# The head of a fused attention and MLP kernel: all first loads on one queue, w1 in smaller pieces, two transposed tiles copied in halves, layer 1 in a new order

## The chip, the cores and the metric

One NeuronCore of a Trainium2 chip runs the whole kernel. The metric is the device time of one execution in microseconds (us). The core has TensorE (PE in the profile; its weight loads are PEld), VectorE (DVE), ScalarE (ACT), GpSimd (POOL) and SyncE (SP), which does nothing here but issue DMAs. ACT and POOL can issue DMAs too, each on a queue of its own. Every engine runs its own list of instructions in order; they wait for each other by semaphores.

## The reference

Two branches read the same layer-normalised input, and their sum is added to it. The sequence has S = 2048 rows of D = 448; there are 16 heads of 28 features, and the hidden layer has 1792 features; all tensors are bf16.

```
xn  = layernorm(x)
# A: linear attention with a softmax feature map
q, k, v = split(xn @ wqkv)                        # 16 heads of 28
phi(t)  = concat(softmax(t @ w_phi), softmax(-t @ w_phi))
kv, z   = sum_s phi(k)^T v,  sum_s phi(k)
A       = (phi(q) @ kv) / (phi(q) @ z + 1e-6) @ wo
# B: MLP
B       = silu(xn @ w1) @ w2
out     = x + A + B
```

## The kernel before

The rows are cut into 16 tiles of 128. A tile is normalised on DVE: statistics (`bnst`, L690, then `bnag`, L691), the reciprocal of the standard deviation (`ve` and `rstd`), and the scaling itself (`xn`, L705). For tiles 0 to 3 `ve` is a square root on ACT (L694) and `rstd` a reciprocal on DVE (L696); for the later tiles both are on POOL (L699, L701). The normalised tile must be transposed, since TensorE contracts over partitions. Tiles 0 to 3 are transposed by TensorE (`tr`, L525) into PSUM and copied to `xnT` (`ev`): by ACT (L531) for tiles 0 to 2, by DVE (L535) for tile 3. Tile 0 goes in two halves (`tr0a`/`ev0a` and `tr0`/`ev0`). Tiles 4 to 15 are transposed two at a time by DMA (`xnT_dma5`, `xnT_dma7` ... `xnT_dma15`, L613), issued by SP once DVE has written both tiles of the pair.

Layer 1 of the MLP makes blocks F0 to F27. A block is 256 hidden features (two PSUM banks) by 512 rows (four tiles); F0 to F6 are the seven feature pairs of tiles 0 to 3, and F25 belongs to tiles 12 to 15. Block F*n* with *n* below 7 needs columns 256*n* to 256*n*+255 of w1. The contraction over 448 is three full steps of 128 (the third differs between the two banks) and a rest of 64, which the two banks share. The first three blocks are made tile by tile as tiles come in, in 128x128 matmuls (the "head"); a word such as `20` is block F2 on tile 0, `00a` the first two steps of block F0 on tile 0 and `00b` its third. After the head the blocks' rests (`r0`, `r1`, `r2`) and whole blocks follow in the order of the string `PLAN` (L361), `aF3` and `bF3` being the halves of F3, `av4` a value projection of tiles 4 and 5, and so on. TensorE's order is that string to the end of the kernel, word for word; the other engines' order comes from a list scheduler (`schedule`) with estimated durations, and where a `chain` is written out, from that.

The loads of the start are all listed at L590 to L610. SP issues the x tiles (`x0`, `x1`, `x2` for tiles 2 and 3, `x4` for 4 to 7, `x8`, `x12`), the pieces of w1, wv and then the transposing DMAs of wqkv (`wT_dma`). The first 512 columns of w1 come as two DMAs: contraction steps 0 and 1 (`w1_0`) and the other two (`w1_0r`). The next columns come as three steps and a last one, so `w1_512` and `w1_512r`, `w1_1024` and `w1_1024r`; `w1_512` is on ACT's queue, behind the small activation that loads ACT's first table, and its last step is on SP's. In the profile w1 carries the name of the buffer that holds it, `phT<-in_B_w_dram`. POOL issues four small DMAs of w_phi (`Wp`), from which it then builds two masked blocks (`bdphi`, L620, and `bd0`, L624) before or between the `ve` and `rstd` of tile 4.

What orders the head is written out: TensorE by this list, ACT by a chain, and DVE by another chain that the change leaves alone.

```
chain("bnst0 bnag0 bnst1 bnag1 rstd0 xn0a xn0 rstd1 xn1 bnst2 bnag2 bnst3 bnag3 rstd2 xn2 rstd3 xn3 ev3".split())
chain("warm_act w1_512 ve0 ve1 ev0a ev0 ev1 ve2 ve3 ev2 silu_table".split())
for word in "tr0a tr0 tr1 00a 10a 01a 11a 00b 10b 01b 11b tr2 20 21 tr3 02 12 22 03 13 23".split():
```

Ahead of the head TensorE runs 38 matmuls on a constant (L574) that nothing reads.

Of the kernel before, what the change touches and what calls it, by code (L numbers as in the profile page):

```python
# [140 lines left out]
class _Prog:  # L141
# [86 lines left out]
    def schedule(self, stalls=()):  # L228
# [53 lines left out]
        while done < n:  # L282
# [78 lines left out]
PLAN = """r0 aF3@4 r2 r1 bF3 aF6@0 aF4@6 bF6 bF4 aF5@4 av2@2 av0@0 bv2 bF5 av4@6 bv0 bv4 aF10@2 aF9@0 bF10 f0@6 bF9 aF12@4 aF7@2  # L361
# [9 lines left out]
def bass_parallel_sum__linear_kernel_hedgehog__dense_activation_silu__prompt_kernel(  # L371
# [36 lines left out]
    with es:  # L408
# [171 lines left out]
        def load_x(t0, t1):  # L580
            load(x_sb[:, t0:t1, :], rows_of(A_x, t0, t1), f"x{t0}", lat=1400.0)
# [7 lines left out]

        load_x(0, 1)  # L590
        load_x(1, 2)
        load_x(2, 4)
        load(w1_sb[:, 0:2, 0:512], B_w1[0:256, 0:512].rearrange("(k p) f -> p k f", p=128), "w1_0")
        load(w1_sb[:, 2:4, 0:512], bass.AP(B_w1.tensor, B_w1.offset + 256 * FF, [[FF, 128], [64 * FF, 2], [1, 512]]), "w1_0r")
        load_w1(512, 1024, "act")
        load_x(4, 8)
        load_w1(1024, FF)
        load_rows4(wv_sb, A_wqkv, 2 * D, 3 * D, "wv")
        load_x(8, 12)
        load_x(12, 16)  # L600
# [86 lines left out]
        def ln_tile(t):  # L687
# [26 lines left out]
                          xn_sb[:, sl - 1:sl + 1, :].rearrange("p i c -> p (i c)"), 950.0, f"xnT_dma{t}", 1330.0, lat=850.0)  # L714
                return

            def turn_over(k0, k1, b, tag):
                tps = bank16[b][:, 128 * k0:128 * k1].rearrange("p (k c) -> p k c", k=k1 - k0)
                transposes([(tps[:, kt - k0, :], xn_sb[:, sl, KS[kt]:KS[kt] + 128]) for kt in range(k0, k1)], f"tr{tag}")
                if t < 3:  # L720
                    act(dstx[:, k0:k1, :], tps, ACTF.Identity, 128 * (k1 - k0), f"ev{tag}")
                else:
                    copy(dstx[:, k0:k1, :], tps, 128 * (k1 - k0), f"ev{tag}")
# [299 lines left out]

        head = [F(0, 0), F(1, 2), F(2, AUX)]
        seq = []
        for word in "tr0a tr0 tr1 00a 10a 01a 11a 00b 10b 01b 11b tr2 20 21 tr3 02 12 22 03 13 23".split():
            if word[0] == "t":
                seq.append(word)
                continue
            f, t = int(word[0]), int(word[1])  # L1030
            n0 = len(P.ops)
            head[f][0](t * 128, t * 128 + 128, {"": (0, 1, 2), "a": (0, 1), "b": (2,)}[word[2:]])
            for n, o in enumerate(P.ops[n0:]):
                o.name = f"F{word}_{n}"
                seq.append(o.name)
# [204 lines left out]
```

## Time and profile before

| | |
|---|---|
| time, median of 3 runs | 146.54 us (146.45 to 146.69) |
| span of the profiled execution, first to last instruction | 145.1 us |
| PE busy | 141.6 us (98%) |
| DVE, ACT, POOL busy | 89.5, 79.4, 75.1 us |
| granted TensorE clock | 1.00 throughout |
| DMA moved | 17.59 MB, 121 GB/s over the span |

The profile is of one execution; its own time is known as its span, and the timed runs lie 1.4 us above that, for what comes before the first and after the last instruction. A row of the timeline gives the start, the length, the engine, the line and operation, `out<-in`, the number of instructions merged, and in brackets how long the engine was idle before and what ended that. Matmuls are pipelined, so a row's start says more than its length. Times are in us from the span's start.

### The profile page before, as it was taken

How to read it: one execution, taken by the hardware profiler on the slowest of the kernel's cores; microseconds unless marked ns; L12 is line 12 of the kernel's file. 1: busy time of each engine (PE TensorE's matmuls, PEld its weight loads, DVE VectorE, ACT ScalarE, POOL GpSimd, SP SyncE). 2: the span in 40 equal slices, each digit the busy share in tenths (PEclk: the TensorE clock that was granted, in tenths of full speed). 3: DMA queues.
4: the chain of work that ended last, by engine and by line, in shares of the span. 5: the costliest groups of instructions: out<-in, count | busy, mean ns of one | idle time of the engine just before them, and what ended most of it. 6: DMA issues, size and time to landing. Idle time of an engine off the chain costs nothing.

```text
span 145.1 us, 4509 instructions
## 1 busy us (share of the span) xinstructions
PE 141.6 (98%) x1947; PEld 83.6 (58%) x1947; DVE 89.5 (62%) x195; ACT 79.4 (55%) x96; POOL 75.1 (52%) x93
## 2 busy tenths in 40 slices
PE   7999999999999999999999999999999999999994
PEld 7895444445444544476787655565555555555663
DVE  1969898600760069939049999927796384625822
ACT  4567856479995999979887949228620000000000
POOL 8808567620197008799935999991497600000000
PEclk9999999999999999999999999999999999999999
DMA  4999998746970000000000069959889999633432
GB/s 101 347 346 266 283 153 119 147 87 139 356 203 5 0 2 5 0 0 5 0 5 5 0 88 195 124 108 181 76 164 164 214 193 167 134 74 72 133 127 63
DMA packets 44500, 17.59 MB, mean 121 GB/s; under 512 B 37040, under 2 KB 44096, under 8 KB 44480
## 3 DMA queue, kind: packets, MB, share of 16 engines
q1 hardware_dynamic: 41648, 15.10, 52.7%
q10 hardware_dynamic: 2704, 2.17, 5.3%
q8 instruction: 15, 0.25, 0.8%
q14 instruction: 5, 0.04, 0.1%
q0 software_dynamic: 128, 0.03, 0.1%
HBM read 6.57 MB, written 1.84 MB: 58 GB/s over the span
## 4 chain that ended last, share of the span: by engine, by line
PE 93%; DMA 3%; SPq 1%; DVE 0%; issue 0%
PE psum L508 93%; DMA phT<-in_B_w_dram 3%; SPq L545 1%; PE psum L525 0%; DVE x_sb L988 0%
## 5 line engine op out<-in xcount | busy, mean ns | idle before, releaser
L508 PE MATMUL psum<-xnT,phT 64*128 64x512 bf16 (+1 forms) x428 | 46.9, 350 | 0.3 <-ACT xnT L531 0.2
L508 PE MATMUL psum<-w_sb,hT 64*128 64x448 bf16 (+2 forms) x434 | 46.1, 343 | 0.0
L825 DVE TENSOR_REDUCE Rec<-Ek_sb 128x32 f32<-128x896 bf16 (+1 forms) x20 | 24.4, 1251 | 19.0 <-ACT Ek_sb L531 19.0
L531 ACT ACTIVATE hT<-psum 128x1024 bf16<-128x1024 f32 x28 | 27.7, 1023 | 11.2 <-PE psum L508 11.0
L508 PEld LDWEIGHTS psum<-xnT,phT 64*128 64x128 bf16 (+1 forms) x428 | 22.5, 95 | 18.5 <-ACT vaug L531 0.6
L508 PEld LDWEIGHTS psum<-w_sb,hT 64*128 64x128 bf16 (+1 forms) x434 | 23.2, 94 | 17.2 <-issue 0.2
L861 POOL TENSOR_TENSOR RA<-Ek_sb,Rec 128x896 bf16<-128x896 bf16 x16 | 27.1, 1724 | 6.1 <-DVE Rec L826 5.0
L508 PE MATMUL psum<-Wqk,xnT 64*128 64x432 bf16 x224 | 24.4, 343 | 0.0
L531 ACT ACTIVATE Ek_sb<-psum 128x864 bf16<-128x864 f32 x24 | 20.3, 915 | 5.9 <-PE psum L508 3.7
L835 POOL TENSOR_TENSOR Ek_sb<-Ek_sb,Rec 128x896 bf16<-128x896 bf16 x8 | 13.4, 1699 | 17.7 <-DVE Rec L826 17.6
L508 PEld LDWEIGHTS psum<-Wqk,xnT 64*128 64x128 bf16 x224 | 11.2, 95 | 8.1
L531 ACT ACT_TABLE_LOAD x11 | 14.1, 1283 | 1.7 <-PEq L1225 0.8
L835 POOL TENSOR_TENSOR phT<-phT,Rec 128x896 bf16<-128x896 bf16 x8 | 13.4, 1699 | 1.2 <-issue 0.9
L988 DVE TENSOR_TENSOR x_sb<-psum,x_sb 128x448 bf16<-128x448 f32 (+1 forms) x13 | 7.2, 584 | 9.1 <-PE psum L508 9.1
L508 PE MATMUL psum<-wv,xnT 64*128 64x448 bf16 x112 | 12.2, 349 | 0.0
L690 DVE BATCH_NORM_STATS2 st<-x_sb 128x6 f32<-128x448 bf16 x16 | 9.6, 603 | 2.9 <-DMA x_sb<-in_A_x_dram 2.9
L508 PE MATMUL psum<-wo_sb,vaug 64*128 64x448 bf16 (+1 forms) x102 | 10.7, 338 | 0.0
L705 DVE TENSOR_SCALAR RA<-x_sb,mv,rstd 128x384 bf16<-128x384 bf16 (+4 forms) x29 | 9.0, 348 | 1.6 <-POOL rstd L701 1.5
L967 DVE TENSOR_TENSOR vaug<-psum,rden 128x448 bf16<-128x448 f32 x16 | 9.2, 619 | 0.0
L825 DVE TENSOR_REDUCE Rec<-phT 128x64 f32<-128x1792 bf16 x4 | 8.0, 1990 | 1.9 <-ACT phT L531 1.9
L826 DVE RECIPROCAL Rec<-Rec 128x32 f32<-128x32 f32 (+1 forms) x24 | 8.8, 396 | 0.2
L508 PEld LDWEIGHTS psum<-wv,xnT 64*128 64x128 bf16 x112 | 5.3, 94 | 5.6 <-ACT vaug L531 0.5
(60 smaller groups left out, 109.7 us busy)
## 6 DMA issues: line engine op xcount, KB each, us to landing
out_dram<-x_sb ACTq DMA_DIRECT2D x15, 112.0 KB, 2.4
w_sb<-in_B_w_dram SPq DMA_DIRECT2D x1, 1568.0 KB, 7.9
x_sb<-in_A_x_dram SPq DMA_DIRECT2D x3, 448.0 KB, 6.0
wo_sb<-in_A_wo_dram SPq DMA_DIRECT2D x2, 336.0 KB, 7.5
phT<-in_B_w_dram SPq DMA_DIRECT2D x1, 576.0 KB, 7.0
phT<-in_B_w_dram SPq DMA_DIRECT2D x2, 256.0 KB, 4.4
phT<-in_B_w_dram ACTq DMA_DIRECT2D x1, 384.0 KB, 4.6
wv<-in_A_wqkv_dram SPq DMA_DIRECT2D x1, 336.0 KB, 7.2
```

Source lines behind the costliest of these rows:

```text
L508: r = e.matmul(dst, lhsT, rhs, start=st, stop=sp, skip_group_check=True)
L531: P.op("act", d_act(n), lambda e: e.activation(dst, src, func, scale=scale), reads=[src], writes=[dst], table=table, name=name, **keys)
L545: P.dma(lambda e: e.dma_start(out=dst, in_=src), n / 280.0, writes=[dst], name=name, eng=eng, lat=lat)
L690: P.op("dve", 590, lambda e: e.bn_stats(st6[:, t, :], xs), reads=[xs], writes=[st6[:, t, :]], name=f"bnst{t}", okeys_w=["ln"])
L705: P.op("dve", dur, lambda e: e.tensor_scalar(dst, x_sb[:, t, c0:c1], mv[:, t, 0:1], rstd[:, t:t + 1], ALU.subtract, ALU.mult), reads=[xs, ...
L825: P.op("dve", 50 + 967 * n, lambda e: e.tensor_reduce(R2, E4, AXL.X, ALU.add), reads=[E4], writes=[R2], name="Ssum")
L826: P.op("dve", 135 + 210 * n, lambda e: e.reciprocal(R2, R2), reads=[R2], writes=[R2], name="Rrec")
L835: P.op("pool", 1700, lambda e: e.tensor_tensor(E3, E3, Rk[:, :, None].broadcast_to([128, 32, DH]), ALU.mult), reads=[E3, Rk], writes=[E3], ...
L861: P.op("pool", 1700, lambda e: e.tensor_tensor(dst, Eq, Rq.rearrange("p (c j) -> p c j", c=CC)[:, :, :, None].broadcast_to([128, CC, 4, DH ...
L967: P.op("dve", 620, lambda e: e.tensor_tensor(o3, U3[:, :, 0:DH], rden[:, uq, :, None].broadcast_to([128, H, DH]), ALU.mult), reads=[U3[:, ...
L988: P.op("dve", d_dve(cs.stop - cs.start), lambda e: e.tensor_tensor(res[:, cs], ob, addend[:, cs], ALU.add), reads=[ob, addend[:, cs]], wri ...
```

## The change

The loads: `w1_0` is issued ahead of `x2` instead of behind it, `w1_512` moves from ACT to SP, and the columns of w1 from 512 on come in pieces of 256, 512 and 512 columns instead of 512 and 768. Each piece is two DMAs, so SP issues three DMAs more than before, all ahead of wv, x8 and the transposing DMAs; ACT issues one less. The copies out of PSUM of tiles 1 and 2 are cut in two (steps 0 and 1, then 2 and 3), and ACT's chain places `ve2` and `ve3` between them. TensorE's list does the third step of tile 0 before tile 1, puts `tr3` between `20` and `21`, and takes tile 2 by halves. In `PLAN` the blocks F4, F5, F6 come in that order instead of F6, F4, F5, in the same banks. The `lat` values are estimates for the scheduler. As built, the order of DVE is unchanged; on POOL `bd0` now stands ahead of tile 4's `ve` instead of behind it; TensorE has the same instructions in the new order.

```
-PLAN = """r0 aF3@4 r2 r1 bF3 aF6@0 aF4@6 bF6 bF4 aF5@4 av2@2 av0@0 bv2 bF5 ...
+PLAN = """r0 aF3@4 r2 r1 bF3 aF4@0 aF5@6 bF4 bF5 aF6@4 av2@2 av0@0 bv2 bF6 ...
...
         load_x(0, 1)
         load_x(1, 2)
+        load(w1_sb[:, 0:2, 0:512], B_w1[0:256, 0:512].rearrange("(k p) f -> p k f", p=128), "w1_0", lat=1200.0)
         load_x(2, 4)
-        load(w1_sb[:, 0:2, 0:512], ..., "w1_0")
-        load(w1_sb[:, 2:4, 0:512], ..., "w1_0r")
-        load_w1(512, 1024, "act")
+        load(w1_sb[:, 2:4, 0:512], ..., "w1_0r", lat=1200.0)
+        load_w1(512, 768)
         load_x(4, 8)
-        load_w1(1024, FF)
+        load_w1(768, 1280)
+        load_w1(1280, FF)
         load_rows4(wv_sb, A_wqkv, 2 * D, 3 * D, "wv")
...
-            def turn_over(k0, k1, b, tag):
+            def turn_over(k0, k1, b, tag, cut=None):
...
+                for a, b, part in ((k0, k1, ""),) if cut is None else ((k0, cut, "a"), (cut, k1, "")):
+                    if t < 3:
+                        act(dstx[:, a:b, :], tps[:, a - k0:b - k0, :], ACTF.Identity, 128 * (b - a), f"ev{tag}{part}")
...
-                turn_over(0, 4, (7, 4, 5)[t - 1], str(t))
+                turn_over(0, 4, (7, 4, 5)[t - 1], str(t), 2 if t < 3 else None)
...
-        chain("warm_act w1_512 ve0 ve1 ev0a ev0 ev1 ve2 ve3 ev2 silu_table".split())
-        byname = {o.name: o for o in P.ops}
-        byname["w1_512"].deps.add(byname["warm_act"].id)
-        byname["w1_512"].odeps -= byname["w1_512"].deps
+        chain("warm_act ve0 ve1 ev0a ev0 ev1a ve2 ev1 ve3 ev2a ev2 silu_table".split())
...
-        for word in "tr0a tr0 tr1 00a 10a 01a 11a 00b 10b 01b 11b tr2 20 21 tr3 02 12 22 03 13 23".split():
+        for word in "tr0a tr0 tr1 00a 10a 00b 10b 01a 11a 01b 11b tr2 20 tr3 21 02a 12a 22a 02b 12b 22b 03 13 23".split():
```

More of the change, by code (lines that the diff above doesn't have):

```diff
@@ L360 @@
           ("pool", "pe"): 100.0}
-PLAN = """r0 aF3@4 r2 r1 bF3 aF6@0 aF4@6 bF6 bF4 aF5@4 av2@2 av0@0 bv2 bF5 av4@6 bv0 bv4 aF10@2 aF9@0 bF10 f0@6 bF9 aF12@4 aF7@2
+PLAN = """r0 aF3@4 r2 r1 bF3 aF4@0 aF5@6 bF4 bF5 aF6@4 av2@2 av0@0 bv2 bF6 av4@6 bv0 bv4 aF10@2 aF9@0 bF10 f0@6 bF9 aF12@4 aF7@2
 aF11@0 f1@6 bF11 bF7 bF12 aF25@0 ak2@6 bF25 bk2 av8@4 av12@2 bv8 ak0@0 bv12 bk0 av10@6 aF22@4 bv10 aF17@2 bF22 av14@6
@@ L591, in bass_parallel_sum__linear_kernel_hedgehog__dense_activation_silu__prompt_kernel @@
         load_x(1, 2)
+        load(w1_sb[:, 0:2, 0:512], B_w1[0:256, 0:512].rearrange("(k p) f -> p k f", p=128), "w1_0", lat=1200.0)
         load_x(2, 4)
-        load(w1_sb[:, 0:2, 0:512], B_w1[0:256, 0:512].rearrange("(k p) f -> p k f", p=128), "w1_0")
-        load(w1_sb[:, 2:4, 0:512], bass.AP(B_w1.tensor, B_w1.offset + 256 * FF, [[FF, 128], [64 * FF, 2], [1, 512]]), "w1_0r")
-        load_w1(512, 1024, "act")
+        load(w1_sb[:, 2:4, 0:512], bass.AP(B_w1.tensor, B_w1.offset + 256 * FF, [[FF, 128], [64 * FF, 2], [1, 512]]), "w1_0r", lat=1200.0)
+        load_w1(512, 768)
         load_x(4, 8)
-        load_w1(1024, FF)
+        load_w1(768, 1280)
+        load_w1(1280, FF)
         load_rows4(wv_sb, A_wqkv, 2 * D, 3 * D, "wv")
@@ L715, in ln_tile @@
                 return
-            def turn_over(k0, k1, b, tag):
+            def turn_over(k0, k1, b, tag, cut=None):
                 tps = bank16[b][:, 128 * k0:128 * k1].rearrange("p (k c) -> p k c", k=k1 - k0)
                 transposes([(tps[:, kt - k0, :], xn_sb[:, sl, KS[kt]:KS[kt] + 128]) for kt in range(k0, k1)], f"tr{tag}")
[L720 to L723, printed above, removed]
+                for a, b, part in ((k0, k1, ""),) if cut is None else ((k0, cut, "a"), (cut, k1, "")):
+                    if t < 3:
+                        act(dstx[:, a:b, :], tps[:, a - k0:b - k0, :], ACTF.Identity, 128 * (b - a), f"ev{tag}{part}")
+                    else:
+                        copy(dstx[:, a:b, :], tps[:, a - k0:b - k0, :], 128 * (b - a), f"ev{tag}{part}")
             if t == 0:
```

## The prediction

> **What bounds the kernel now.** I read the page's busy time first, then the chain of work that ended last in order of time, then the timeline of the first 10 us, then the DMAs of the start by queue. Page, and the chain (start, length, what):
>
> ```profile
> span 145.1 us, 4509 instructions
> ...
> PE 141.6 (98%) x1947; PEld 83.6 (58%) x1947; DVE 89.5 (62%) x195; ACT 79.4 (55%) x96; POOL 75.1 (52%) x93
> ...
> PE 93%; DMA 3%; SPq 1%; DVE 0%; issue 0%
> ```
>
> ```profile
> 2.68 5.04 DMA phT<-in_B_w_dram
> 7.71 0.04 issue
> 7.76 0.62 PE psum L508 x8
> 8.38 0.22 PE psum L525 x4
> 8.60 0.67 PE psum L508 x12
> 9.27 0.22 PE psum L525 x4
> 9.50 30.98 PE psum L508 x345
> 40.48 0.01 issue
> 40.48 102.59 PE psum L508 x1503
> ```
>
> The reader is to see that TensorE has no hole from 7.76 to 143.1 and that the same instructions run after the change. So the time falls by as much as TensorE reaches its gapless stretch earlier, unless something later then makes it wait. What starts that stretch is one DMA, issued at 2.68 and landed at 7.71: w1_0r. The timeline of the head shows the rest:
>
> ```profile
> 5.70 0.35 PEld L525 LDWEIGHTS psum<-ident,RA 128*128 128x128 bf16 x4 [0.24 <-DVE RA L705]
> ...
> 7.00 0.45 PEld L508 LDWEIGHTS psum<-xnT,phT 128*128 128x128 bf16 x8 [0.38 <-ACT xnT L531]
> ...
> 7.37 0.40 DVE L705 TENSOR_SCALAR RA<-x_sb,mv,rstd 128x448 bf16<-128x448 bf16 x1
> ...
> 7.75 0.45 PEld L508 LDWEIGHTS psum<-xnT,phT 128*128 128x128 bf16 x8 [0.30 <-DMA phT<-in_B_w_dram]
> 7.87 0.40 DVE L705 TENSOR_SCALAR RA<-x_sb,mv,rstd 128x448 bf16<-128x448 bf16 x1
> 8.16 0.27 PEld L525 LDWEIGHTS psum<-ident,RA 128*128 128x128 bf16 x4
> ```
>
> TensorE stands still for tile 1's copy (until 7.00) and for w1_0r (until 7.75). The weights of tr2 are loaded at 8.16 though xn2 was done at 7.37+0.40 = 7.77. So the two waits together cost 0.4 us: what tr2 comes later than its own input allows.
>
> **Why w1_0r lands at 7.71.** The DMAs by queue between 5.0 and 5.5 (packets, MB, share; q1 is SP's, q10 ACT's):
>
> ```profile
> q10 hardware_dynamic: 164, 0.17, 96.1%
> q1 hardware_dynamic: 16, 0.01, 7.8%
> ```
>
> For half a microsecond ACT's w1_512, which nobody needs before 8.4, pushed SP's queue aside. From 6 to 7, with ACT's done, SP's queue alone moved 0.36 MB in a microsecond.
>
> **The change, part by part.** Landings of before are issue start plus the median to landing: x2 1.74+2.7 = 4.4, w1_0 5.9, w1_512 6.9, w1_0r 7.7, w1_512r 8.1, x4 9.7, w1_1024 11.2.
>
> *Loads.* On one queue 704 KB now lie up to the end of x2 and 960 KB up to the end of w1_0r. For x2: from below, 448 KB were there at 4.4 and 256 KB more at 0.36 MB/us take 0.7: 5.1; from above, the 704 KB of before were there at 5.9, with ACT's traffic between. DVE comes to bnst2 at 5.57, so the cost is 0 to 0.35; I take 0, since ACT's traffic is what goes. For w1_0r: 5.1+0.7 = 5.8 from below, the unchanged 7.7 from above; I take 5.9. For w1_768r, 2176 KB: between 1920 KB at 9.7 and 2496 KB at 11.2 it is 10.4; aF3 wants it at 11.67−0.40 = 11.27, so nothing is waited for. Rest of w1: 2688 KB, 11.7 as before, wanted by aF5 after 13.
>
> *TensorE and ACT.* 00a starts at 6.11 behind tr1, as now. Matmuls of 128 columns follow each other at 0.056 us (chain: 12 in 0.67). 00a and 10a are 8: 6.64. 00b and 10b need ev0 (the ACT row 5.55+1.40 holds ev0a, ev0, ev1; ev0 ends at 6.21) and w1_0r (5.9): 4 matmuls, 6.86. 01a and 11a need ev1a, which starts at 6.35 as ev1 does now and takes 0.38 like ev0a: 6.73. 8 matmuls, 7.31. 01b and 11b need ev1's second half: ev1a 6.35, ve2 6.63, ev1 6.84 to 7.22 (an instruction on ACT starts 0.1 before the end of the one ahead: a half takes 0.28 of it, a ve 0.2): 7.53. Then tr2 waits for xn2 until 7.76 and starts at 7.82, by tr1's distance of 0.056 from its xn1. Before it started at 8.22. **Gain 0.40.** xn2 itself cannot move: DVE's chain is unchanged, and rstd2 follows bnag3 (6.95+0.18 = 7.13), not ve2.
>
> From tr2 to the end of the head 56 matmuls at 0.056 stand on both sides. tr3, now ten matmuls behind tr2, comes at 8.38; xn3 ends at 8.27 and allows 8.32: no wait, by 0.05. ev2a and ev2 (8.25 and 8.53, 0.38 each) are there for 8.93 and 9.60. A tile in two halves takes ACT 0.28+0.28 instead of 0.50, so 0.06 more, hidden in the 1.18 us that it is idle before ev2. ACT's DMA issue of 0.43 lay in 1.53 us of idleness: 0.
>
> *SP's three more issues* at 0.47 (the median of its w1 issues) put wT_dma4 and all behind it 1.4 us later. The landing need not follow: wT_dma4 was issued by 8.5 and landed at 15.4 (8.1 after its start), so the data queue was 7 us behind the issues. Cost between 0 and 1.4 for xnT_dma5; I take 0, nearest to that row. The issue of wv moves 1.4 too; it is wanted at 16.9 and landed at 12.7.
>
> *POOL.* bd0 ahead of ve4 makes rstd4 0.05 later (bdphi ends 11.17, bd0 0.27, ve4 0.23, against 11.60 now); from below, tile 4's statistics come 0.4 earlier with ev3. The LN chain thus moves by +0.05 to −0.4; I take +0.05, as bdphi waits for Wp and that row I leave:
>
> ```profile
> 10.61 0.56 POOL L620 TENSOR_TENSOR BD<-Wp,mask_half 128x224 bf16<-128x224 bf16 x1 [3.88 <-DMA Wp<-in_A_w_phi_dram]
> ```
>
> The next fixed date is xnT_dma15, landed at 25.80+3.8 = 29.6; aF25 loads its weights at 29.90 and multiplies at 30.12, in the new kernel at 29.50 and 29.72. After w1_0r's landing TensorE needed 0.05; 29.65+0.05 = 29.70, just in time: 0 (at most 0.2). *F4, F5, F6* have equal durations: 0.
>
> **Sum** on the profiled span: 145.13 − 0.40 = 144.73. The median of the runs is 1.41 above the span: 146.54 − 0.40 = **146.14**.
>
> **The rivals.**
> 1. *x2 too late.* At its upper bound of 5.9 DVE's chain, and with it tr2, moves 0.35; the gain is 0.05: 146.5. The same is left if aF25 or another fixed date takes 0.2 back (146.35). For it: x2 now lies behind 256 KB. Against: ACT's 384 KB are gone.
> 2. *w1_0r not earlier* (the other side). It is now needed by 00b, at 6.64, ahead of all of tile 1. If it still lands at 7.71, the 16 matmuls from 00b to 11b start at 7.76, take 0.89, and tr2 comes at 8.65: 0.43 slower, 146.97. It decides from a landing at 7.28 on; up to 6.88 it costs nothing. Against: the queue rows above. The Trainium skill, "DMA: Bandwidth & Descriptors", section "Issuing engines are not separate DMA queues", says that DMAs of all issuing engines run on the same 16 engines and interleave, and that a second issuing engine saves issue time alone. By that rule alone the move to SP wins nothing at the landing; the trace agrees on the sharing, but its 164 packets to 16 show that who shares matters.
> 3. *SP late.* If all 1.4 us reach xnT_dma5, it lands at 18.9+1.4 = 20.3; av4 starts at 20.03−0.40 = 19.63, waits 0.7, and the kernel is 0.3 slower: 146.85.
> 4. *Small pieces.* If a piece carries a cost of its own on the queue, w1_768r is late: aF3 has 11.27−10.4 = 0.87 to spare. x0 and x1 landed 0.48 apart (2.87 and 3.35), the two pieces of wv 0.3 apart, the later of each 112 KB. If each of the three extra pieces cost a whole 0.48, aF3 would wait 1.44−0.87 = 0.57: 146.7; with the difference, 0.18 each, nothing waits. The Trainium skill, same page, section "Bandwidth", asks for DMAs of 1 MiB and gives 0.95 us for one of 64 KB; by that an estimate is 3x0.95−0.87 = 2.0 of waiting and 148.1. The 0.3 us of wv's second piece, which lay in a full queue as these do, disagrees.
>
> **How the numbers follow.** The forecast has 0.56, rival 1 0.20, rival 2 0.12, rival 3 0.08, rival 4 0.03; 0.01 is for no change at all. A measurement of this kernel tells about 0.2% (0.29 us) from no change. The forecast's own range is 146.0 to 146.3, and 0.03 of its 0.56 is within 0.2%. Rival 1 is within it for 0.15 and faster for 0.05; rivals 2 and 3 are slower but for 0.02 near the deciding point; rival 4 is slower for 0.01. Faster 0.58, same 0.23, slower 0.19. The range goes from 145.9 (the forecast less the 0.24 by which runs differ) to 146.85, rival 3; the later landings of rival 2 and what lies below 145.9 are left out.
>
> **What would show it.** In the profile after: w1_0r and x2 landed before 6.6 and 5.6; no DMA in the head's chain of waits but the x loads; PEld waiting for DVE before tr2, at 7.8 instead of 8.16; one gapless PE from there; wv and xnT_dma5 landed as before. Wrong it would be made by x2's statistics starting after 5.6, a PE gap before 00b, aF3, av4 or aF25.

## The result, and the profile after

| | kernel before | changed kernel |
|---|---|---|
| median of the runs made side by side | 147.22 us (146.33 to 148.40) | 147.94 us (147.16 to 149.22) |
| ratio, 95% interval | | 1.0061 (1.0033 to 1.0088) |
| span of the profiled execution | 145.1 us | 147.8 us (its time: 149.01) |
| PE busy | 141.6 us | 141.9 us |

The change makes the kernel 0.6% slower; a gain of 0.40 us had been forecast, from 146.54 to 146.14. Runs of either kernel spread over some 2 us and the median of the kernel before moves between 146.4 and 147.2 from one set of runs to the next, so every ratio below is against runs of the kernel before in the same set. The ratio is not the quotient of the two medians, and can lie up to 0.3% beside it.

On the page of the changed kernel, the shares of the span in the chain of work that ended last (before, PE had 93% of it):

```profile
PE 85%; DMA 8%; SPq 4%; DVE 1%; issue 1%
```

The chain itself (start, length, what):

```profile
5.19 7.88 DMA phT<-in_B_w_dram
13.08 0.14 issue
13.21 28.82 PE psum L508 x308
...
133.76 4.29 DMA vaug<-vaug
138.05 0.14 issue
138.19 7.53 PE psum L508 x62
```

TensorE does the same work, but it is no longer the chain from 7.76 on. Two DMAs stand in it: w1_768r, issued at 5.19 and landed at 13.08, and the last transposing DMA of the kernel, 4.29 us long. The timeline of the start says what the head itself did:

```profile
4.11 0.63 DVE L691 BATCH_NORM_STATS2 st<-x_sb 128x6 f32<-128x448 bf16 x1 [0.44 <-DMA x_sb<-in_A_x_dram]
...
6.25 0.63 DVE L691 BATCH_NORM_STATS2 st<-x_sb 128x6 f32<-128x448 bf16 x1
...
8.36 0.23 PEld L525 LDWEIGHTS psum<-ident,RA 128*128 128x128 bf16 x4 [0.34 <-DVE RA L706]
...
11.63 0.56 POOL L621 TENSOR_TENSOR BD<-Wp,mask_half 128x224 bf16<-128x224 bf16 x1 [4.93 <-DMA Wp<-in_A_w_phi_dram]
...
12.62 0.23 POOL L700 TENSOR_SCALAR ve<-mv 128x1 f32<-128x1 f32 x1 [0.19 <-DVE mv L692]
...
13.21 0.61 PE L508 MATMUL psum<-xnT,phT 64*128 64x512 bf16 x4 [1.23 <-DMA phT<-in_B_w_dram]
```

x2's statistics start at 6.25 instead of 5.57, so tr2 comes at 8.36 and not at 7.82. Most of these 0.68 us are not x2's: x1, whose issue the change leaves at 1.3, is in at 4.08 instead of 3.35, so DVE starts tile 1's statistics at 4.11 instead of 3.65 and has scaled tile 1 some 0.48 later; x2, in at 6.23, adds the other 0.20. aF3 stands still until 13.2. bdphi on POOL starts a microsecond later than before (11.63 against 10.61), and here tile 4's ve waits longer still, until 12.62, for the statistics of x4, which is in at 11.66 instead of 9.69.

I followed the same matmul through both traces. The changed kernel's TensorE is 0.15 us behind at the end of the head, 1.54 after aF3, stays there until 130, and is 2.65 behind at the end. 2.65 is far more than the 0.72 between the medians, so one pair of profiles could not settle what the change costs.

### The profile page after: what moved, and what is told of

The parts are those of the page before. It is cut to its first block, busy times and chain, and to the rows that moved or that the text cites. A ratio compares the mean times of both kernels' runs of the same rounds, so it can differ in the third digit from the quotient of the medians.

```text
span 147.8 us, 4516 instructions
## 1 busy us (share of the span) xinstructions
PE 141.9 (96%) x1947; PEld 84.4 (57%) x1947; DVE 89.6 (61%) x195; ACT 79.8 (54%) x98; POOL 75.1 (51%) x93
## 3 DMA queue, kind: packets, MB, share of 16 engines
q10 hardware_dynamic: 2304, 1.78, 4.6%
## 4 chain that ended last, share of the span: by engine, by line
PE 85%; DMA 8%; SPq 4%; DVE 1%; issue 1%
PE psum L508 85%; DMA phT<-in_B_w_dram 5%; DMA vaug<-vaug 3%; SPq L545 3%; SPq L614 1%; DVE vaug L969 0%; DVE x_sb L990 0%; DVE rden L964 0%; DVE den L962 0%; SPq L1193 0%
## 5 line engine op out<-in xcount | busy, mean ns | idle before, releaser
L827 DVE TENSOR_REDUCE Rec<-Ek_sb 128x32 f32<-128x896 bf16 (+1 forms) x20 | 24.4, 1251 | 18.9 <-ACT Ek_sb L531 18.9
L508 PEld LDWEIGHTS psum<-xnT,phT 64*128 64x128 bf16 (+1 forms) x428 | 23.2, 95 | 18.7 <-DMA phT<-in_B_w_dram 1.5
L531 ACT ACTIVATE Ek_sb<-psum 128x864 bf16<-128x864 f32 x24 | 20.3, 916 | 6.6 <-issue 3.2
L508 PEld LDWEIGHTS psum<-Wqk,xnT 64*128 64x128 bf16 x224 | 11.2, 95 | 8.2
```

The source lines that it names most:

```text
L508: r = e.matmul(dst, lhsT, rhs, start=st, stop=sp, skip_group_check=True)
L531: P.op("act", d_act(n), lambda e: e.activation(dst, src, func, scale=scale), reads=[src], writes=[dst], table=table, name=name, **keys)
L827: P.op("dve", 50 + 967 * n, lambda e: e.tensor_reduce(R2, E4, AXL.X, ALU.add), reads=[E4], writes=[R2], name="Ssum")
```

## The experiments

Two tables sum up all profiles; the experiments below refer to them. The first says when the loads of the start were in. A DMA is spread over 16 engines; "last" is when the last of its 16 parts was in, which is what a waiting engine sees, "middle" is the ninth of the 16. "Old loads" are the eight profiles with the loads as before (the kernel before twice, e1, e6, e7, e16, e18, e20), "new loads" the six with exactly the loads of the change (the changed kernel twice, e2, e5, e15, e17). Of Wp's four DMAs bdphi needs the first three and bd0 the fourth. Times in us:

| | old loads, last | new loads, last | new loads, middle | forecast for new |
|---|---|---|---|---|
| x2 | 4.36 to 4.79 | 5.20 to 6.23 | 5.01 to 5.54 | 5.1 to 5.9 |
| w1_0r | 7.58 to 8.49 | 6.80 to 7.32 | 5.91 to 6.51 | 5.9 |
| the piece with aF3's columns | 7.93 to 8.91 | 11.14 to 13.08 | 10.33 to 10.87 | 10.4 |
| Wp, all four | 10.63 to 11.24, once 12.26 | 11.36 to 12.24 | | as before |
| xnT_dma5: issued | 14.28 to 15.28 | 15.49 to 17.43 | | |
| xnT_dma5: in | 18.86 to 20.54 | 19.48 to 21.05 | | 18.9 |

The second says where TensorE lost time: how much the same matmul lags behind the first profile of the kernel before, split by where the lag arose (head; wait for w1_768r at aF3; wait for xnT_dma5 at av4, near 21; wait at the fold, near 28, that is, ahead of the second group of matmuls that read the masked blocks (`f1` in `PLAN`; the first, `f0`, comes near 24); wait for the last transposing DMA, near 137). "Both cures" are bdphi later on POOL and wider idle matmuls, each explained with its experiment:

| profile | head | aF3 | av4 | fold | last DMA | sum |
|---|---|---|---|---|---|---|
| before, again (e14) | 0.26 | 0 | 0 | 0.01 | 0.79 | 1.05 |
| changed | 0.15 | 1.39 | 0 | 0.01 | 1.10 | 2.65 |
| changed, again (e13) | -0.26 | 0 | 0 | 0.50 | 1.06 | 1.29 |
| e1 new order, old loads | 0.59 | 0 | 0 | 0 | 0.78 | 1.38 |
| e2 new loads, old order | 0.13 | 0.14 | 0.05 | 0.31 | 0.96 | 1.58 |
| e3 x4 behind w1_768 | -0.44 | 0 | 0.28 | 1.01 | 1.04 | 1.89 |
| e4 larger pieces of w1 | 1.30 | 0 | 0 | 0 | 0.77 | 2.07 |
| e5 changed, 37 idle matmuls | 0.24 | 0 | 0.91 | 0.02 | 1.02 | 2.19 |
| e6 before, 39 idle matmuls | 0.07 | 0 | 0 | 0 | 1.19 | 1.26 |
| e7 = e1, 37 idle matmuls | 0.38 | 0 | 0 | 0.01 | 1.02 | 1.41 |
| e9 = e4, 37 idle matmuls | 0.70 | 0 | 0.06 | 0.01 | 0 | 0.77 |
| e11 w1_512 on ACT | 0.07 | 0.01 | 0 | 0.88 | 0.82 | 1.78 |
| e12 x4 split | 0.33 | 0 | 0 | 1.07 | 0.95 | 2.34 |
| e15 changed, bdphi later | -0.39 | 0.85 | 0 | 0.01 | 0.87 | 1.34 |
| e16 before, wide idle matmuls | 0.17 | 0 | 0.47 | 0.01 | 0 | 0.65 |
| e17 changed, both cures | -0.24 | 0.39 | 0.88 | 0.01 | 0 | 1.03 |
| e18 before, POOL late | 0.78 | 0 | 0 | 0.18 | 0 | 0.95 |
| e19 = e17, w1_512 on ACT | -0.45 | 0 | 0.06 | 0.01 | 0.13 (124.6, not the DMA) | -0.25 |
| e20 before, both cures | -0.02 | 0 | 0 | 0 | 0 | -0.01 |

### The two halves of the change alone

**e1_order_only**: the kernel before with the new TensorE list, the halved copies and ACT's new chain; loads and PLAN as before.

```
-for word in "tr0a tr0 tr1 00a 10a 01a 11a 00b 10b 01b 11b tr2 20 21 tr3 02 12 22 03 13 23".split():
+for word in "tr0a tr0 tr1 00a 10a 00b 10b 01a 11a 01b 11b tr2 20 tr3 21 02a 12a 22a 02b 12b 22b 03 13 23".split():
-chain("warm_act w1_512 ve0 ve1 ev0a ev0 ev1 ve2 ve3 ev2 silu_table".split())
+chain("warm_act w1_512 ve0 ve1 ev0a ev0 ev1a ve2 ev1 ve3 ev2a ev2 silu_table".split())
```

> The kernel before, with the new list of TensorE's head, the copies of tiles 1 and 2 in halves and ACT's chain to match; the loads and their queues, and the order F6, F4, F5, as before. Theory A (the loss is TensorE's wait ahead of aF3, 1.4 us in the profile of the changed kernel, because the columns 768 to 1023 of w1 now come behind x4): no wait ahead of aF3, since they lie in w1_512 as before; but 00b now needs w1_0r, which lands near 7.7, so 16 matmuls run from 7.76 and tr2 starts at 8.65 instead of 8.22: 0.4 us slower, ratio 1.003. Theory B (the new order or the halves cost the time): ratio 1.006 as for the whole change.

Measured: 147.77 us, ratio 1.0053 (1.0026 to 1.0080). In its timeline TensorE stands before 00b, which now comes ahead of tile 1:

```profile
7.89 0.41 PEld L508 LDWEIGHTS psum<-xnT,phT 128*128 128x128 bf16 x7 [1.16 <-ACT ve L694]
7.92 0.50 PE L508 MATMUL psum<-xnT,phT 128*128 128x128 bf16 x6 [1.01 <-DMA phT<-in_B_w_dram]
```

The weight load's releaser is named as an ACT instruction, the matmul's as the DMA; w1_0r landed at 7.78, so it is the DMA. The order without earlier loads loses 0.59 in the head.

**e2_loads_only**: the changed kernel with the old list, whole copies and ACT's old chain (without w1_512).

```
-for word in "tr0a tr0 tr1 00a 10a 00b 10b 01a 11a 01b 11b tr2 20 tr3 21 02a 12a 22a 02b 12b 22b 03 13 23".split():
+for word in "tr0a tr0 tr1 00a 10a 01a 11a 00b 10b 01b 11b tr2 20 21 tr3 02 12 22 03 13 23".split():
-turn_over(0, 4, (7, 4, 5)[t - 1], str(t), 2 if t < 3 else None)
+turn_over(0, 4, (7, 4, 5)[t - 1], str(t))
```

> The changed kernel with the old list of TensorE's head, whole copies of tiles 1 and 2 and ACT's old chain; loads and PLAN of the changed kernel. Theory A: the wait ahead of aF3 stays, 1 to 1.4 us, and the ratio is that of the whole change, 1.004 to 1.009. Theory B: the loss is gone, ratio 0.998 to 1.001.

Measured: 147.89 us, 1.0062 (1.0034 to 1.0090). The loads alone cost as much as the whole change. So does the order alone, within the intervals: the two halves do not add up. The wait of 1 to 1.4 us at aF3 that theory A expected is 0.14 here; in this profile the loss is made of small waits, this one and 0.31 at the fold among them.

### The order and the size of the pieces on SP's queue

**e3_x4_behind**: the changed kernel with x4 behind the piece that aF3 needs.

```
-        load_x(4, 8)
         load_w1(768, 1280)
+        load_x(4, 8)
```

> The changed kernel with x4 (448 KB) issued behind the piece of columns 768 to 1279 instead of ahead of it. Theory A: w1_768r lands 1.2 to 1.4 us earlier than the 13.1 of the changed kernel, TensorE waits 0.2 us or less ahead of aF3; x4 lands 1.4 us later, so tiles 4 to 7 are normalised later and av4 may wait up to 1 us: ratio between 0.998 and 1.006, with the wait moved. Theory C (the rows of 512 bytes in the 256-column piece slow the queue, wherever x4 stands): w1_768r still lands after 12.3 and aF3 waits 0.5 us or more.

Measured: 147.87 us, 1.0058 (1.0027 to 1.0090). The head gains 0.44 and aF3 waits for nothing (w1_768r in at 10.23), but tiles 4 to 7 are normalised later, and the fold waits instead. Chain of this profile:

```profile
5.25 6.18 DMA x_sb<-in_A_x_dram
...
27.07 1.04 DVE Wqk L684 x2
...
28.16 1.89 PE psum L508 x29
```

So aF3's wait of 1.4 us can go and the time stays: something else costs as much. The theory that aF3 alone is the loss falls here.

**e4_wide_rows**: the pieces of w1 behind w1_0r larger again, all on SP's queue.

```
-        load_w1(512, 768)
+        load_w1(512, 1024)
         load_x(4, 8)
-        load_w1(768, 1280)
-        load_w1(1280, FF)
+        load_w1(1024, FF)
```

> The changed kernel with the columns from 512 on cut as before, 512 to 1023 and 1024 to 1791, all on SP's queue, x4 between the two. No row is under 1024 bytes, and F3's weights lie ahead of x4 again. Theory A and theory C both expect no wait ahead of aF3; w1_512r by 8.5; what the change promised then shows: tr2 at 7.8 to 8.3, ratio 0.997 to 1.001. Theory C adds that the queue moves 0.33 MB a microsecond or more between 6 and 7.5, where the changed kernel moved 0.25. Theory D (one queue instead of two is too slow for x2 and w1_0r): x2's statistics start after 6.0, tr2 at 8.3 or later, ratio 1.000 or above.

Measured: 148.10 us, 1.0066 (1.0038 to 1.0094). Both theories had 0.997 to 1.001. w1_512 is in at 9.58 and the head waits for it: 1.30 lost. Fewer, larger pieces do not mend it; on one queue the larger first piece holds up the head.

### Is the last wait a matter of one instruction more or less?

The wait for the last transposing DMA stood in all five profiles of changed code so far, and not in the one of the kernel before. Its place in TensorE's list differed (3795 before, 3796 or 3797 after), and the idle matmuls at the start move it.

```
-for i in range(38):
+for i in range(37):      # e5: changed kernel, e7: e1, e9: e4; in e6, the kernel before: range(39)
```

> The changed kernel with 37 instead of 38 matmuls on the constant ahead of the head: TensorE's list is two instructions shorter, weight load and matmul, and all that follows stands two places earlier. Theory E: most of the loss is not in the head. In the profiles of the changed kernel and of the four variants TensorE waits 0.8 to 1.1 us near 137 for the last transposing DMA of the attention output, which takes 4.0 to 4.3 us from issue to landing there and 2.45 in the kernel before; in the kernel before the 16384-byte packet of the instruction queue near 135.6 starts after that DMA's landing, in the variants during it. The wait for that DMA is instruction 3795 of TensorE's list before (a weight load and its matmul counted as two), 3797 in the changed kernel, 3796 or 3797 in the variants, because each has one or two more wait instructions in its head; the fetch is set off by the place in the list. So with the place back at 3795: landing 2.4 to 2.6 us after issue, no wait above 0.2 us there, 0.7 to 1.1 us faster than the changed kernel, ratio to before 0.998 to 1.002. Theory A (all of the loss is the wait ahead of aF3): the tail wait comes and goes by itself, ratio unchanged at 1.004 to 1.009.

> The kernel before with 39 instead of 38 matmuls on the constant, nothing else: the wait for the last transposing DMA of the attention output stands at 3797, as in the changed kernel. Theory E: that DMA takes 3.8 to 4.3 us to land, TensorE waits 0.7 to 1.1 us ahead of the last W block, ratio 1.004 to 1.008. Theory A: one matmul of 0.1 us in a time when TensorE waits for the first tile anyway, ratio 1.000 to 1.001.

> The variant with the new order and halves alone, loads as before, with 37 matmuls on the constant: the place of the wait is 3794. Theory E: no tail wait; what is left is the head, where 00b waited for w1_0r until 7.92 and TensorE was 0.6 us behind the kernel before: ratio 1.000 to 1.004, 0.7 us below the same variant with 38. Theory A: as with 38, 1.003 to 1.008.

> The variant with all loads on one queue and columns 512 to 1023 and 1024 to 1791 as the pieces, with 37 matmuls on the constant: the place of the wait is 3794. Theory E: no tail wait, 0.7 us or more below the same variant with 38: ratio 0.998 to 1.003, and if w1_512r lands before 8.3 this is the variant that could be faster than both. Theory A: as with 38, 1.004 to 1.009.

Measured: e5 148.21 us, 1.0083 (1.0053 to 1.0113); e6 147.43, 1.0038 (1.0008 to 1.0068); e7 147.57, 1.0049 (1.0016 to 1.0083); e9 147.83, 1.0087 (1.0051 to 1.0122). The place in the list does not decide: e5 stands at 3795, e7 and e9 at 3794; e5 and e7 wait, e9 does not, and e6, the kernel before at 3797, waits 1.19. But e6 shows that the wait belongs to the kernel before as well.

### Two queues, and x4 in two

**e11_act_quarter**: the changed kernel with w1_512's first three steps (256 columns) on ACT's queue. **e12_x4_split**: tiles 4 and 5 ahead of w1_768, tiles 6 and 7 behind it.

```
-        load_w1(512, 768)
+        load_w1(512, 768, "act")                                      # e11
-        load_x(4, 8)
+        load_x(4, 6)                                                  # e12
         load_w1(768, 1280)
+        load_x(6, 8)
```

> The changed kernel, but the first three steps of w1_512 (256 columns, 192 KB) are issued by ACT on its own queue behind its first table load, as in the kernel before (there with 512 columns). Theory of the single queue (early on, one queue moves fewer bytes in a half microsecond than two do, so everything behind w1_0r comes late): w1_512 is in by 7, x4 and w1_768r land 0.5 to 1.5 us earlier than in the changed kernel's profile (11.66 and 13.08), aF3 waits under 0.5 us, and by 35 us TensorE is 0 to 0.6 behind the kernel before. Theory of the prediction (ACT's traffic is what makes w1_0r late): w1_0r lands 0.3 us or more behind where the changed kernel has it (7.01), and 00b waits. If both hold, the wait only moves from aF3 to 00b. A wait of 0.8 to 1.1 us ahead of the last output projections may come on top, whichever holds.

> The changed kernel, but x4 is cut in two: tiles 4 and 5 stay ahead of the w1 piece of 768 to 1279, tiles 6 and 7 go behind it. Theory of the queue's order: the piece for aF3 now has 112 KB x 2 less ahead of it and tile 4 still comes early enough for the layer norm, so neither aF3 (1.4 us in the changed kernel) nor the fold (1.0 us with the whole of x4 behind) waits more than 0.3; by 35 us TensorE stands -0.4 to +0.3 against the kernel before. Rival, that the landings are late and uneven as such and the order only chooses who waits: some wait of 0.5 us or more before 35 us remains (aF3, av4 or the fold), and TensorE is 0.6 or more behind by then. Time by the first: 146.3 to 146.8 where the tail has no wait, about 1 us more where it has; by the rival: 147.3 to 148.2.

Measured: e11 147.49 us, 1.0025 (0.9991 to 1.0059); e12 148.06, 1.0067 (1.0035 to 1.0100). In neither does aF3 wait, in both the fold does, 0.88 and 1.07, so that e11 is 0.96 behind by 35 us, more than the theory of the single queue allowed. e12's order theory falls: the wait stays, in another place. In e12 it is in part tiles 6 and 7, which are in at 12.06 and whose layer norm is late besides.

### Both kernels a second time

**e13_new_again** and **e14_old_again** have no edit.

> The changed kernel as it is, a second profile. If aF3's wait of 1.4 us for w1_768r belongs to the change, it is there again, between 1.0 and 1.6, and the TensorE is 1.3 to 1.7 behind the kernel before by 35 us. If the place of the late landing is chance, another wait has its place (av4, the fold) or it is under 0.6. Ahead of the last output projections: a wait of 0.8 to 1.1 us or none.

> The kernel before as it is, a second profile. Up to 130 us it lies within 0.15 of the first one. At the last transposing DMA: if the wait of about 1 us there belongs to the kernel before as much as to the variants, it shows in this profile in about half of the cases, with a time near 147.4; if it is brought about by the change, there is none, and the time is 146.2 to 146.8.

Measured: 147.68 and 147.44 us, one run each. The second profile of the changed kernel has no wait at aF3 (w1_768r was in at 11.14, last of 16; in the first profile at 13.08). So that wait is not fixed; what is there instead is the fold, and its chain goes back to Wp:

```profile
5.16 5.78 DMA Wp<-in_A_w_phi_dram
...
11.11 0.56 POOL BD L621
11.67 0.23 POOL BD L625
11.90 0.23 POOL ve L700
12.20 0.58 POOL rstd L702
...
26.46 1.04 DVE Wqk L684 x2
...
27.55 2.54 PE psum L508 x35
```

POOL makes the masked blocks before tile 4's ve and rstd. Wp is late, so bdphi, rstd4, the layer norm of the following tiles on DVE, and the fold's first subtractions (Wqk) that stand behind it on DVE are late; `f1` needs the two PSUM banks that these read. From rstd4's start to that of `f1` it is 15.35 us here, 15.25 in e2, 15.33 in e11: a date. In the kernel before rstd4 starts at 11.60, which puts that date at 26.9, and TensorE came at 27.3: 0.4 to spare.

The second profile of the kernel before has the last wait too: its last transposing DMA, issued at 132.44, takes 4.01 us.

### The fold's wait taken away, and put where it was not

**e15_new_bd_later**: the changed kernel with bdphi and bd0 behind rstd7 on POOL. **e18_old_pool_late**: the kernel before with two memsets between bdphi and tile 4's ve.

```
+        chain("rstd7 bdphi bd0 ve8".split())                          # e15
...
+        memset(KVm[:], 0.0, 464, "pad0")                              # e18
+        memset(KVm[:], 0.0, 464, "pad1")
+        chain("bdphi pad0 pad1 ve4".split())
```

> The changed kernel, with POOL's two products that make the masked blocks (bdphi and bd0, which wait for Wp) behind rstd7 instead of ahead of tile 4's ve. Theory of the fold: in the second profile of the changed kernel, and in those with x4 split, with ACT's quarter and with the loads alone, rstd4 starts at 12.2 to 12.9 because bdphi waits for Wp, and the fold starts 15.3 us behind rstd4 and makes TensorE wait 0.3 to 1.1 near 28. With bdphi out of the way rstd4 starts at x4's pace, the wait near 28 goes (under 0.1), and what TensorE has lost by 35 us is what it had lost after aF3: -0.4 to +0.2, or up to 1.5 where aF3 has to wait for its piece of w1. Median 0.3 to 0.6 us below the changed kernel's. Rival: the fold waits for other work of DVE; then the wait stays, and so does the median. The wait of about 1 us ahead of the last output projections is not touched.

> The kernel before, with two memsets of 0.47 us each put on POOL between bdphi and tile 4's ve: the loads as they were, tile 4's layer norm 0.94 us later. Theory of the fold: rstd4 starts at 12.5 instead of 11.6, the fold near 27.85 instead of 27.3, and TensorE waits 0.4 to 0.6 us there, with nothing lost ahead of it; by 35 us it is 0.4 to 0.6 behind, and the median is up by as much. Rival, that there is more to spare: nothing is lost, and a later Wp can't be what the changed kernel loses.

Measured: e15 147.66 us, 1.0030 (0.9999 to 1.0062); e18 147.69, 1.0059 (1.0025 to 1.0093). e15, timeline: tile 4's ve now waits for its statistics, not for Wp, and the fold's wait is gone; this time aF3 waited.

```profile
11.46 0.23 POOL L700 TENSOR_SCALAR ve<-mv 128x1 f32<-128x1 f32 x1 [4.82 <-DVE mv L692]
...
12.13 1.24 PE L508 MATMUL psum<-xnT,phT 64*128 64x512 bf16 x9 [0.69 <-DMA phT<-in_B_w_dram]
```

e18, timeline: POOL, and the fold 15.33 behind rstd4.

```profile
11.49 1.02 POOL L538 MEMSET KVm<- 128x464 bf16 x2
...
12.94 0.57 POOL L701 TENSOR_TENSOR rstd<-ve,neghalf 128x1 f32<-128x1 f32 x1
...
28.26 0.09 PEld L508 LDWEIGHTS psum<-BD,Y_sb 64*128 64x128 bf16 x1 [0.53 <-DVE Wqk L683]
```

The date holds with the old loads. Only 0.18 of it shows as a wait, since w1_0r came late in this execution (8.49) and the head had lost 0.78 already; but the sum by 35 us is the date's, 0.96, and the median rose by 0.9 (147.69 against 146.79). More than the 0.4 to 0.6 expected: rstd4 came at 12.94, not 12.5. A tile 4 normalised this late, as late as in any profile of the changed kernel (rstd4 at 12.20 to 12.94), is thus enough for a loss of the size seen. That bdphi's place gains the changed kernel anything does not show in its times: the ratio goes from 1.0061 to 1.0030, but the intervals overlap, and by the medians e15 stands 0.87 above the kernel before in its set and the changed kernel 0.72 in its own. It is the profiles that carry this.

### The last wait moved

**e16_old_wide_warm**: the kernel before with 10 idle matmuls of 512 columns for 38 of 128. **e17_new_bd_wide**: e15 with the same edit.

```
-        for i in range(38):
+        for i in range(10):
-            ... e.matmul(banks[3][:, 0:128], ones_bf[:], ones_bf[:], ...
+            ... e.matmul(banks[3][:, 0:512].rearrange("p (r c) -> p r c", r=4), ones_bf[:],
+                         ones_bf[:, None, :].broadcast_to([128, 4, 128]), ...
```

> The kernel before, with its 38 idle matmuls of 128 columns at the start made as 10 of 512 columns. The work is nearly the same in length, but TensorE's list has 28 matmuls less, so that every later instruction stands that much nearer to the list's start. Theory of the fetch (the last transposing DMA takes 4.0 to 4.4 us instead of 2.4 when a packet of 16384 bytes of TensorE's own list passes while it is under way): the packet that came at 134.2 to 135.6 comes some 1.5 to 2 us later, behind that DMA's landing, the DMA takes 2.4 to 2.5, the wait of 0.8 to 1.2 us is not there, and the runs lie at 146.2 to 146.8 nearly all, median 146.4. Rival, that the slow DMA is chance or belongs to the output transfers around it: it takes 4 us or more in this profile too or in half of the runs, and the median stays at the kernel before's.

> The changed kernel with both: bdphi and bd0 behind rstd7, and 10 idle matmuls of 512 columns for the 38 of 128. If both theories hold (the fold's wait comes from Wp over POOL, the last wait from the fetch of TensorE's list), neither wait is in the profile, and what is left against the kernel before is the head and aF3: 146.0 to 146.8 where aF3 needs not wait, up to 147.9 where it does; median at or below the kernel before's. If neither holds, it lies where the changed kernel lies, 0.7 to 0.9 above.

Measured: e16 146.41 us, 0.9964 (0.9932 to 0.9996), faster than both kernels by an interval that only just leaves out 1; e17 147.04, 0.9999 (0.9960 to 1.0038). The DMAs by queue (packets, MB, share) in the 2.46 us after the last transposing DMA's issue, first the kernel before of e14, then e16; the last line of each gives the median us to landing:

```profile
q8 instruction: 1, 0.02, 2.3%
...
vaug<-vaug SPq DMA_TRANSPOSE x1, 4.0
```

```profile
q1 hardware_dynamic: 1039, 0.25, 52.3%
q10 hardware_dynamic: 60, 0.05, 8.1%
...
vaug<-vaug SPq DMA_TRANSPOSE x1, 2.5
```

One packet of 16384 bytes, of a queue that the profile calls instruction, makes the difference: in e16 it comes at 136.94, after the landing at 135.30, and the answer there has no line of that queue. Of all 20 profiles, 13 have this packet while the DMA is under way, and it takes 3.99 to 4.42 us; 7 have it later, and it takes 2.41 to 2.47. No profile is between. In eight of the 13, fifteen of the DMA's sixteen parts are in within 2.48 us and only the last is late. In e18 the packet came later without any edit for it, in e9 with one idle matmul less, which did not help e5 and e7, and in the kernel before once so and once not: that much is chance. e16, e17, e19 and e20, with the shorter list, all have it later.

The shorter list moves the packets, it does not take them away, and the last DMA is not the only one that they meet. In e16, e19 and e20 one of them is under way together with xnT_dma5, which then takes 5.47 to 5.58 us; in the other 17 profiles none is, and it takes 3.46 to 4.20. That is e16's wait at av4: xnT_dma5 is issued 0.16 later than in the first profile of the kernel before and is in 1.68 later. The packet among the DMAs from its issue at 14.95 to its landing at 20.54 in e16:

```profile
q8 instruction: 1, 0.02, 1.3%
```

In e17 neither the fold nor the last DMA costs anything, and against before the changed kernel stands even. What is left in its profile is aF3, 0.39, and av4, 0.88. av4 waits for xnT_dma5, which is in at 20.93. SP's issue of it and the one ahead in e17, DVE's write of tile 5 in e17, and SP's two issues in the kernel before:

```profile
14.18 3.13 SPq L614 DMA_TRANSPOSE Y_sb<-in_A_wqkv_dram  x1
17.35 2.68 SPq L614 DMA_TRANSPOSE xnT<-RA  x2
```

```profile
13.37 0.60 DVE L706 TENSOR_SCALAR RA<-x_sb,mv,rstd 128x384 bf16<-128x384 bf16 x2
```

```profile
12.48 2.26 SPq L613 DMA_TRANSPOSE Y_sb<-in_A_wqkv_dram  x1
14.79 2.83 SPq L613 DMA_TRANSPOSE xnT<-RA  x2
```

Tile 5, the second that xnT_dma5 needs, is written at 13.97, but SP, which issues in order, comes to xnT_dma5 at 17.35, at once behind the issue of the transposing DMA ahead of it. (The chain of this profile names DVE's statistics of tile 8 as what released it. They start at 17.09 and last 0.63, so they are not over at 17.35.) So it is in 19 of the 20 profiles: SP goes from one issue to the next without a pause, and xnT_dma5 follows the one ahead by at most 0.05 us. (e18 is the other: there SP waits 0.26 for tile 5.) With three issues more ahead of it xnT_dma5 is issued later, in e17 by 2.6 us and in e5 by 2.2. Not all of that is the three issues: those of the transposing DMAs take 1.1 to 3.3 us, as 3.13 here, and why is not seen.

### What is left

**e19_act_bd_wide**: e17 with e11's edit. **e20_old_bd_wide**: the kernel before with both cures, as a control.

> The changed kernel with both cures (bdphi and bd0 behind rstd7, 10 idle matmuls of 512 columns for the 38 of 128) and the first three steps of w1_512 on ACT's queue. With both cures and one queue the changed kernel stood 147.04 against 146.41 for the kernel before with the wide idle matmuls: 0.6 us, seen in that profile as 0.38 at aF3 and 0.89 at av4, both waits for DMAs. Theory that the single queue brings w1's later pieces late: aF3 waits under 0.1 us here, as in the profile with ACT's quarter alone, and the median is 146.3 to 146.6. Rival, that these landings are late whichever queue issues them: aF3 or av4 waits 0.4 us or more, and the median is 146.8 to 147.2.

> The kernel before with both cures, as a control: loads, order and copies as they were. In the kernel before with the wide idle matmuls alone Wp came late once too (bdphi at 11.32, rstd4 at 12.57), and xnT_dma5, which follows tile 4 and 5, made av4 wait 0.47. If the place of bdphi matters with the old loads as well, av4's wait is gone and the median is 146.1 to 146.4; if the old loads mostly leave enough to spare, it is what it was, 146.4, within 0.1.

Measured: e19 146.31 us, 0.9991 (0.9964 to 1.0019); e20 146.31, 0.9994 (0.9964 to 1.0024). In these runs the kernel before itself stood at 146.43. e19's profile shows the head as it was forecast. Timeline:

```profile
7.14 0.40 DVE L706 TENSOR_SCALAR RA<-x_sb,mv,rstd 128x448 bf16<-128x448 bf16 x1
...
7.77 0.39 PE L525 MATMUL psum<-ident,RA 128*128 128x128 bf16 x4
```

tr2 at 7.77 instead of 8.22, and no wait for a DMA behind it but 0.06 at av4. aF3 waits for nothing, as the theory of the single queue had it. But in this profile nearly every load was early (x4 at 8.72, no other new profile under 9.5), and e19's interval and e17's overlap widely, so the medians do not separate one queue from two. The landings do, in the middle: up to the last piece of w1 the same 2688 KB of x and w1 are loaded in every kernel, and that piece's ninth part is in at 11.13 to 11.55 in the ten profiles with a piece of w1 on ACT's queue and at 11.69 to 12.29 in the ten with all on SP's. So w1 comes later with one queue; whether the queue itself is slower or SP, with one issue more to make, issues later, no run separates. And it does not decide aF3 alone: by the last part, e11 has its piece only at 11.59.

e20 shows no gain over the kernel before in its set, though it has e16's edit: e16's gain did not come a second time. Nor does the head's gain show in the times: e19, 0.38 ahead by 35 us in its profile, has the median of e20.

## Why the prediction was wrong

**"TensorE has no hole from 7.76 on, so the time falls by as much as it reaches its gapless stretch earlier, unless something later makes it wait"**: right as a frame; four things did make it wait.

**Gain 0.40 from tr2**: the mechanism and the size are right, -0.39 to -0.45 in e3, e15 and e19, where x1 was in by 3.68 and x2 by 5.20 to 5.61. What failed is the term "x2: I take 0". x2 is in at 5.20 to 6.23, in two of the six profiles (6.21, 6.23) beyond its upper bound of 5.9. e5 is rival 1 pure: DVE stands 0.65 for x2 and the head is 0.24 late. In the first profile tr2 came at 8.36 and the gain was gone too, but there 0.48 of the 0.68 is x1, which the prediction did not look at. x1 is nearly as late in profiles with the old loads (3.97 in e14), so that part is not the change's.

**w1_0r at 5.9**: the middle engine lands it at 5.91 to 6.51, the last at 6.80 to 7.32. In the first profile 00b waited some 0.3 for it, which cost nothing, because tr2 had to wait for tile 2 after that. Rival 2 did not come about in the changed kernel; e1 and e7, which are that rival made, lost 0.59 and 0.38 where its price was 0.43.

**"w1_768r 10.4, nothing is waited for"**: the first step that failed. The last part of the piece came at 11.14 to 13.08, against a date of 11.27. The 10.4 was worked out between two landings of the kernel before, x4 at 9.7 and w1_1024 at 11.2; both are those of the last part, and of one profile. That the ninth part in the changed kernel, at 10.33 to 10.87, comes near it is luck: between the ninth parts of the same two loads (8.77 and 10.66) the same sum gives 9.6. So two things were wrong. All parts come later than the bytes of the kernel before say, the ninth by 0.7 to 1.3; and the last is 0.75 to 2.45 behind the ninth, where in the profile that the sum was taken from it was 0.56 to 0.92 for those two loads. The sum also never said what the edit did to that date's margin: in the kernel before the columns of aF3 were in w1_512, in at 8.1, 3.2 us ahead of that date. Cut at 768 and queued behind x4, they have 0.87 at best.

**"bdphi waits for Wp and that row I leave"**: the second step that failed, and the one that recurs. The row moved. With more of SP's loads ahead of it, all of Wp was in at 11.36 to 12.24 instead of 10.63 to 11.24 (once, in e16, 12.26), and with it rstd4 at 12.20 (e13) to 12.69 (e2) instead of 11.60; in the first profile it was x4 that put rstd4 at 12.94. The term "+0.05 to -0.4" for the layer norm was +0.6 to +1.3; 0.4 of it was spare. All five profiles with the edited loads, bdphi in its old place and no larger delay ahead show the wait (e2, e3, e11, e12, e13; in e3 x4 itself was as late, in e12 tiles 6 and 7 were later still), no profile with bdphi moved does, and e18 makes it with the old loads. That it is SP's traffic that holds Wp is argued from these landings; no run moves Wp alone.

**"SP's three more issues cost 0"**: wrong in some executions. av4 waited 0.91 in e5 and 0.88 in e17, for xnT_dma5 in at 21.05 and 20.93, where 18.9 was forecast and rival 3 had 20.3. This is rival 3, and by its own way: xnT_dma5 is issued when SP comes to it. The argument that the data queue was 7 us behind the issues, so that a landing need not follow its issue, does not hold for xnT_dma5, whose landing follows its issue by 3.5 to 4.1 us in the six profiles.

**xnT_dma15 and aF25, F4 to F6, ACT's extra 0.06**: 0, as forecast.

**Rival 4, small pieces**: a cost of its own per piece is not seen: with the larger pieces of e4 and e9, also on SP's queue alone, the ninth part of w1's last piece is in at 12.19 and 11.69, with the small ones at 11.70 to 12.29. The estimate of 148.1 from the Trainium skill's "DMA: Bandwidth & Descriptors", section "Bandwidth", is near the measured time, but not for its reason: e4, with larger pieces, is no faster (148.10). The section's figure is for DMAs that GpSimd issues; w1 is issued by SP.

**The end of the kernel** was in no step. The last transposing DMA costs about 0.8 to 1.2 us whenever the instruction packet meets it, in the kernel before as well. It is 1.10 of the 2.65 by which the two first profiles differ, where the medians differ by 0.72. It is not what the change costs: with it the changed kernel with bdphi later stands at 1.0030, without it e17 over e16 is 0.9999/0.9964 = 1.0035, where both hold only within their intervals.

So the loss, as far as the profiles show it, is the margins. The head gains up to 0.45, when x1 and x2 are early; the new loads use up what aF3, the layer norm and av4 had to spare, and then one or another of them waits 0.3 to 1.4 us, a different one from run to run. By 35 us the profiles with the new loads and neither cure stand 0.24 to 1.55 behind the first profile of the kernel before, and its second stands 0.27. Not settled are why single engines of the 16 lag by up to 2.75 us, why SP's issues of transposing DMAs take up to 3.3 us, and how much of the late loads is owed to the single queue.

## What to carry to other kernels

A landing worked out by bytes from one profile is one sample: whoever waits gets the last of 16 parts, here 0.1 to 2.75 us behind the ninth, so a margin under a microsecond in a full queue is no margin. A DMA that an engine issues in order behind others comes as late as their issues, whatever its data wait for. When loads are reordered, list every transfer's date and its spare before and after, above all of those on other queues that were not touched, and find what stands behind them on an in-order engine. And take a second profile of the kernel before as of the new one before explaining the difference: here four tenths of the difference between the first two was a wait that both kernels have.

## What the runs showed of the hardware

- A packet of 16384 bytes on the queue named instruction lengthens a transposing DMA that is under way from 2.41 to 2.47 us (7 profiles) to 3.99 to 4.42 (13 profiles). That it is TensorE's own list is inferred from e16, where 28 matmuls less on TensorE put it behind the landing; what holds the DMA meanwhile is not seen. The same holds for xnT_dma5: 5.47 to 5.58 with such a packet (3 profiles), 3.46 to 4.20 without (17). Idle matmuls made wider instead of more numerous gained 0.36% (0.04 to 0.68) in one set of runs and nothing clear of noise in another (e20, 0.9994, which also has bdphi later).
- SP's issues of transposing DMAs take 1.1 to 3.3 us each in the stretch ahead of xnT_dma5, and hold all that SP issues after them.
- One DMA's 16 parts end far apart: x4 in the first profile of the changed kernel has its ninth part in at 8.91, the fifteenth at 10.26 and the last at 11.66. In e19 the same load has 8.25 and 8.72.
- The executions of one kernel differ in which wait they show: the changed kernel lost 1.39 at aF3 in one profile and nothing in the next.
